# A decode attention kernel: most of each V tile's matmuls in a loop with register addresses, V tiles in two pieces of their own

## The chip, the cores and the metric

The kernel runs on one core of a Trainium2 chip. The metric is the time of one execution on the device in microseconds, as the median of several runs. The kernel before takes 2521.05 us, the median of 3 runs from 2520.66 to 2521.23. The profile is of one further execution, which took 2520.96 us; its span, from the first instruction to the last event, is 2519.1 us.

Names used below: TensorE (PE in the profile; PEld is its weight load), VectorE (DVE), ScalarE (ACT), GpSimd (POOL) and SyncE (SP), whose queue issues nearly all transfers here. SBUF is the on-chip memory that transfers write, PSUM the one that TensorE writes.

## The reference

One token goes through an attention block with a cached K and V and through a gated feed-forward block, and a scalar gate mixes the two.

```python
def _A_ref(x, k_cache, v_cache, wq, wo):          # x 1x1x512; caches 1 x 32 x 65536 x 128
    B, Sq, D = x.shape
    H, Dh = 32, 128
    q = (x @ wq).reshape(B, Sq, H, Dh).transpose(0, 2, 1, 3)
    scores = jnp.einsum("bhqd,bhkd->bhqk", q, k_cache) * (Dh ** -0.5)
    p = softmax(scores, axis=-1)
    o = jnp.einsum("bhqk,bhkd->bhqd", p, v_cache)
    return o.transpose(0, 2, 1, 3).reshape(B, Sq, H * Dh) @ wo

def _B_ref(x, w_gate, w_up, w_down):               # F = 1792
    return (silu(x @ w_gate) * (x @ w_up)) @ w_down

g = sigmoid((x * gate_w).sum(-1, keepdims=True))
return g * _A_ref(...) + (1 - g) * _B_ref(...)
```

All inputs are bf16. The two caches are 32 heads x 65536 keys x 128 numbers each, 537 MB apiece; each number is used once.

## The kernel before

**Tiles.** A head's 65536 keys lie as 512 keys on each of 128 partitions. A tile is half of that: 256 keys per partition (SIZE), 128 x 32768 bf16, 8.39 MB in one load. So a head has two K tiles and two V tiles (G = 2), and there are N = 64 of each. The loop over n (line 485) loads K tile n and V tile n-2 (LEAD = 2), in this order on SP's queue.

**A K tile** goes through VectorE in place (`products`, line 249): one multiply with the head's query row, which stands on all partitions (line 258), and three additions that fold the 128 numbers of a key to 16 (line 262: the 64-wide, 32-wide and 16-wide halves). TensorE sums the 16 with eight matmuls against the identity (`scores`, line 267), and VectorE takes the last pair together (`add_up`, line 282). At an even n the head before has all its scores: its maximum (`row_max`, line 299, with a step over ScalarE and TensorE), the exponentials on ScalarE and the weight 1/sum follow (`exponentials`, `weight`). They stand behind the multiply of the first 64 keys of K tile n; the other 192 keys follow as a second piece (cuts, line 497).

**A V tile** is used by `values` (line 335): 64 matmuls, each with four keys' probabilities as weights (128x4) and four keys' V rows (128 x 512) as the moving side. They go in turn to four strips of PSUM at partitions 0, 32, 64 and 96. When a head is complete, ScalarE copies O_ps to SBUF (`head_copy`), TensorE sums the useful rows (`head_sum`), and ScalarE writes the row, weighted, into a row of four heads (`head_row`, line 422). Every four heads, `turn` (line 461) turns the row to columns.

**Slots.** SBUF has three slots of a tile's size (`big0` to `big2`). K and V tiles and at the start and end the weights wq, the feed-forward weights and wo take the slot that came free first (`free`, lines 79 to 84). A K tile frees its slot after its scores (line 280), a V tile after its 64 matmuls (line 349). A load waits on SP's queue until its slot is free, and later loads wait behind it.

**wo.** The rows of wo for heads 0 to 3 are loaded during the run in 40 small loads (`load_tall`, line 395; TALL_LOADS, line 29) and multiplied then (`project_tall`). The others are loaded at the end, around the last two V tiles (lines 545 to 551): heads 4 to 19 ahead of the last V tile, the rest behind it.

**Order.** `manual_schedule()` (line 77) keeps each engine's instructions in the order of the program text. All addresses are constants and every loop is unrolled.

Of the kernel before, what the change touches and what calls it, by code (L numbers as in the profile page):

```python
# [8 lines left out]
ACT = mybir.ActivationFunctionType  # L9
# [6 lines left out]
SLOTS = 3  # L16
# [5 lines left out]
V_CUTS = {63: (0, 168, 232, 256)}  # L22

QUAD = 4
FIRST, LONG, PAIR, LAST = (0, 4), (4, 20), (20, 28), (28, 32)

SHARES = ((5, 3), (3, 15), (1, 4))
TALL_ROUNDS = ((2, 0, 4), (1, 0, 5), (1, 5, 10), (1, 10, 15), (0, 0, 3))
TALL_LOADS = {14: 0, 23: 1, 32: 2, 41: 3, 50: 4}
TALL_PROJECTS = {18: 0, 27: 1, 36: 2, 45: 3, 54: 4}  # L30
# [3 lines left out]
def kernel(  # L34
# [31 lines left out]
    qT = edge.tile([P, H], f32, name="qT")  # L66
    ring = ctx.enter_context(tc.tile_pool(name="ring", bufs=1))
    slots = [f"big{i}" for i in range(SLOTS)]
# [8 lines left out]
    ctx.enter_context(tc.manual_schedule())  # L77

    free = [2, 0, 1]
    taken = {}  # L80

    def big(name):
        slot = free.pop(0)
        return ring.tile([P, SIZE * Dh], bf16, name=name, tag=slots[slot]), slot

    wq_t, wq_slot = big("wq_t")
    wq_sb = wq_t[:, : KT * H * Dh].rearrange("p (t f) -> p t f", t=KT)
    nc.sync.dma_start(out=wq_sb, in_=A_wq.rearrange("(p t) f -> p t f", t=KT))  # L88
    x_row = consts.tile([1, D], bf16, name="x_row", tag="o_row")
    nc.scalar.dma_start(out=x_row, in_=A_x[0])  # L90

    K_tiles, V_tiles, S_tiles, P_tiles, S_parts = {}, {}, {}, {}, {}

    def load(dst, cache, n, name, cuts=None):
        t, taken[name, n] = big(name)
        view = t.rearrange("p (j d) -> p j d", d=Dh)
        src = cache[0, n // G, :, :].rearrange("(p j) d -> p j d", p=P)
        a = n % G * SIZE
        cuts = cuts or (0, SIZE)
        for c, d in zip(cuts[:-1], cuts[1:]):  # L100
            nc.sync.dma_start(out=view[:, c:d, :], in_=src[:, a + c : a + d, :])
        dst[n] = view
# [30 lines left out]
    def query_columns(first, last):  # L133
        q_ps = psum_m.tile([P, last - first], f32, name="q_ps", tag="misc")
        for h in range(first, last):
            for t in range(KT):
                nc.tensor.matmul(
                    q_ps[:, h - first : h - first + 1],
                    lhsT=wq_sb[:, t, h * Dh : (h + 1) * Dh],
                    rhs=xT[:, t : t + 1],  # L140
                    start=(t == 0),
                    stop=(t == KT - 1),
                )
        nc.scalar.activation(out=qT[:, first:last], in_=q_ps, func=ACT.Copy)
# [3 lines left out]
    def query_spread(h):  # L148
        diag_q = consts.tile([P, Dh], bf16, name="diag_q")
        nc.scalar.activation(out=diag_q, in_=ident_b, func=ACT.Copy, scale=qT[:, h : h + 1])  # L150
        qb_ps = psum_m.tile([P, Dh], f32, name="qb_ps", tag="misc")
        nc.tensor.matmul(qb_ps, lhsT=ones_b, rhs=diag_q, start=True, stop=True)  # L152
        q_tiles[h] = pair.tile([P, Dh], bf16, name="q_sb")
        nc.scalar.activation(out=q_tiles[h], in_=qb_ps, func=ACT.Copy)  # L154
# [3 lines left out]
    query_columns(0, 1)  # L158
    query_spread(0)
    query_columns(1, H)  # L160
    free.append(wq_slot)
# [10 lines left out]
    gu_t, gu_slot = ring.tile([P, SIZE * Dh], bf16, name="gu_t", tag=slots[wq_slot]), wq_slot  # L172
    free.remove(wq_slot)
# [5 lines left out]
    gw_row = consts.tile([1, D], bf16, name="gw_row", tag="tall")  # L179
# [69 lines left out]
    def products(n, a, b):  # L249

        K = K_tiles[n][:, a:b, :]
        qb = q_tiles[n // G]
        q_rep = bass.AP(
            tensor=qb.tensor,
            offset=qb.offset,
            ap=[list(qb.ap[0]), [0, b - a], [1, Dh]],
        )
        yield nc.vector.tensor_tensor(out=K, in0=K, in1=q_rep, op=ALU.mult)  # L258
# [75 lines left out]

    def values(n, lo=0, hi=SIZE):
        h = n // G
        a = n % G * SIZE
        for j in range(lo, hi, QUAD):
            strip = 32 * ((a + j) // QUAD % 4)
            nc.tensor.matmul(  # L340
                O_ps[strip : strip + QUAD, :],
                lhsT=P_tiles[h][:, a + j : a + j + QUAD],
                rhs=V_tiles[n][:, j : j + QUAD, :],
                start=(a + j < 4 * QUAD),
                stop=(a + j >= NBH - 4 * QUAD),
            )
        if hi == SIZE:
            del V_tiles[n]
            free.append(taken.pop(("V_t", n)))

    def head_copy():
        O_sb = consts.tile([P, QUAD * Dh], f32, name="O_sb")
        nc.scalar.activation(out=O_sb, in_=O_ps, func=ACT.Copy)  # L353
        return [O_sb[:, c * Dh : (c + 1) * Dh] for c in range(QUAD)]

    def head_sum(h, parts):
        if h >= LAST[0]:
            r_ps = psum_r.tile([P, 1], f32, name="r_ps")
            for c in range(QUAD):
                nc.tensor.matmul(  # L360
                    r_ps, lhsT=parts[c], rhs=pick[:, c : c + 1], start=(c == 0), stop=(c == 3)
                )
            return r_ps
        r_ps = psum_r.tile([1, Dh], f32, name="r_ps")
        for c in range(QUAD):
            nc.tensor.matmul(  # L366
                r_ps, lhsT=pick[:, c : c + 1], rhs=parts[c], start=(c == 0), stop=(c == 3)
            )
        return r_ps


    row0 = 0
    TP = 32 + 4 * SHARES[0][0]
    assert sum(2 * 4 * ports * deep for ports, deep in SHARES) == QUAD * P
    TR = max(b - a for _, a, b in TALL_ROUNDS)
    pieces, bases = [], []
    width = 0
    for ports, deep in SHARES:
        bases.append(width)
        for half in range(2):  # L380
            pieces.append((row0, row0 + 4 * ports * deep, width + 32 * half * deep))
            row0 += 4 * ports * deep
        width += TP * deep
    tallT = consts.tile([TP, sum(deep for _, deep in SHARES)], bf16, name="tallT")
    tall = {}

    def tall_row():
        tall["row"] = consts.tile([1, width], bf16, name="tall_row", tag="tall")
        nc.gpsimd.memset(tall["row"], 0.0)

    def tall_zero():
        tall["sb"] = consts.tile([TP, TR, D], bf16, name="tall_sb", tag="tall")
        nc.gpsimd.memset(tall["sb"], 0.0)

    def load_tall(r, half):
        s, a, b = TALL_ROUNDS[r]
        ports, deep = SHARES[s]
        first = pieces[2 * s + half][0]
        for i in range(4):
            src = bass.AP(  # L400
                tensor=A_wo.tensor,
                offset=A_wo.offset + (first + i * deep + a) * D,
                ap=[[4 * deep * D, ports], [1, (b - a) * D]],
            )
            lo = 32 * half + i
            nc.sync.dma_start(
                out=tall["sb"][lo : lo + 4 * (ports - 1) + 1 : 4, : b - a].rearrange(
                    "p t n -> p (t n)"
                ),
                in_=src,  # L410
            )

    def project_tall(r):
        s, a, b = TALL_ROUNDS[r]
        rows = 32 + 4 * SHARES[s][0]
        at = sum(deep for _, deep in SHARES[:s])
        for t in range(b - a):
            into_row(tallT[:rows, at + a + t : at + a + t + 1], tall["sb"][:rows, t, :])
# [3 lines left out]
    def head_row(h, r_ps):  # L422
# [4 lines left out]
        if h < FIRST[1]:  # L427
            for a, b, at in pieces:
                lo, hi = max(a, h * Dh), min(b, h * Dh + Dh)
                if lo < hi:  # L430
                    nc.scalar.activation(
                        out=tall["row"][:, at + lo - a : at + hi - a],
                        in_=r_ps[:, lo - h * Dh : hi - h * Dh],
                        func=ACT.Copy,
                        scale=gate[0:1, :],
                    )
            return
        if h % QUAD == 0:
            rows[h // QUAD] = consts.tile([1, QUAD * Dh], bf16, name="o_row")
        at = (h % QUAD) * Dh  # L440
        nc.scalar.activation(
            out=rows[h // QUAD][:, at : at + Dh], in_=r_ps, func=ACT.Copy, scale=gate[0:1, :]
        )

    def turn_first():
        t_ps = psum_m.tile([TP, tallT.shape[1]], f32, name="t_ps", tag="misc")
        c = 0
        for s, (ports, deep) in enumerate(SHARES):
            src = tall["row"][:, bases[s] : bases[s] + TP * deep]
            for t in range(deep):  # L450
                nc.tensor.matmul(
                    t_ps[:, c + t : c + t + 1],
                    lhsT=src.rearrange("o (p t) -> o t p", t=deep)[:, t, :],
                    rhs=one_b,
                    start=True,
                    stop=True,
                )
            c += deep
        nc.scalar.activation(out=tallT, in_=t_ps, func=ACT.Copy)

    def turn(g):
        if g == 0:
            turn_first()
            return
        first, last = LONG if g * QUAD < LONG[1] else PAIR
# [154 lines left out]
```

## Time and profile before

| what | value |
|---|---|
| median of 3 runs | 2521.05 us |
| the profiled execution | 2520.96 us, span 2519.1 us |
| VectorE busy | 2185.8 us, 87% |
| TensorE matmuls busy | 698.7 us, 28% |
| ScalarE busy | 95.1 us, 4% |
| read from HBM | 1087.64 MB, 432 GB/s over the span |
| instructions in the profile | 12218 |
| instruction fetch (queue q8) | 42 packets, 0.69 MB |
| mean granted TensorE clock | 0.613 of full speed |

How to read the profile: the page has the busy time of each engine, the span cut in 40 slices with a digit for the busy share of each (9 is 90% or more), and the chain of waits that ended last. A row of the timeline has the start and the duration in us, the engine, the line of the kernel, the operation, the tile that is written and those that are read, the shapes and the count; in brackets stand the idle time before it and what ended it. Rows of the view by form have, after the count, the sum in us, the mean of one in ns and the idle time before. In the shape of a matmul, 128*4 is the weights' and 128x512 the moving side's. SPq is a load being issued on SP's queue, not its transfer.

### The profile page before, as it was taken

To read this page: it belongs to the slowest core of one execution; us is meant where nothing else is said; L and a number is where in the kernel's file an instruction comes from. 1 tells how busy PE (TensorE), PEld (TensorE's weight loads), DVE (VectorE), ACT (ScalarE), POOL (GpSimd) and SP (SyncE) were. 2 spreads that over 40 slices of the span, in tenths; PEclk is the share of its full clock that TensorE was granted. 3 is DMA by queue.
4 is the path that set the end of the run, shared out by engine and by line. 5 is a ranking of instruction groups with operands and counts; after the bars stand their busy time and mean duration, and the time that the engine had idled before them with its cause. 6 is when DMAs were issued, how large, how long until landed. Compare 5 with 4: busy or idle time off the path is not lost.

```text
span 2519.1 us, 12218 instructions
## 1 busy us (share of the span) xinstructions
PE 698.7 (28%) x5422; PEld 252.0 (10%) x5422; DVE 2185.8 (87%) x599; ACT 95.1 (4%) x277; POOL 4.0 (0%) x8
## 2 busy tenths in 40 slices
PE   2132222223222222232222322322323223223224
PEld 2010000101001000010000100110100001001011
DVE  6998998888988889888899888898888988889984
ACT  0000000000000000000000000000000000000000
POOL 0000000000000000000000000000000000000000
PEclk9566556656566566665665665656555666656566
DMA  9999999999999999999999999999999999999998
GB/s 419 435 433 433 437 437 433 432 433 435 432 433 434 434 433 433 435 434 433 434 437 432 432 433 433 434 433 434 434 434 433 434 434 433 434 436 432 432 432 378
DMA packets 20875, 1088.41 MB, mean 432 GB/s; under 512 B 2396, under 2 KB 2912, under 8 KB 3416
## 3 DMA queue, kind: packets, MB, share of 16 engines
q1 hardware_dynamic: 20822, 1087.65, 99.7%
q8 instruction: 42, 0.69, 0.1%
q14 instruction: 9, 0.07, 0.0%
q10 hardware_dynamic: 2, 0.00, 0.0%
HBM read 1087.64 MB, written 0.00 MB: 432 GB/s over the span
## 4 chain that ended last, share of the span: by engine, by line
DMA 84%; PE 14%; DVE 1%; issue 0%; SPq 0%; ACT 0%; DVEq 0%
DMA V_t<-in_A_v_cache_dram 81%; PE O_ps L340 14%; DMA wo_t<-in_A_wo_dram 2%; DMA K_t<-in_A_k_cache_dram 1%; DVE K_t L258 1%; DVE K_t L262 1%; PE part_ps L271 0%; PE b_ps L227 0%; SPq L88 0%; ACT out_sb L588 0%; PE a_ps L186 0%; PE g_ps L231 0%; DVEq L258 0%
## 5 line engine op out<-in xcount | busy, mean ns | idle before, releaser
L258 DVE TENSOR_TENSOR K_t<-K_t,q_sb 128x8192 bf16<-128x8192 bf16 (+4 forms) x97 | 1107.3, 11416 | 245.2 <-DMA K_t<-in_A_k_cache_dram 245.2
L262 DVE TENSOR_TENSOR K_t<-K_t 128x4096 bf16<-128x4096 bf16 (+8 forms) x291 | 1001.5, 3441 | 9.0
L340 PE MATMUL O_ps<-V_t,P_sb 128*4 128x512 bf16 x4096 | 365.5, 534 | 923.9 <-DMA V_t<-in_A_v_cache_dram 923.8
L271 PE MATMUL part_ps<-K_t,ident_b 128*128 128x512 bf16 x512 | 230.6, 605 | 611.1 <-DVE K_t L262 611.1
L340 PEld LDWEIGHTS <-P_sb 128*4 128x4 bf16 x4096 | 122.7, 110 | 1160.7 <-issue 1075.5
L271 PEld LDWEIGHTS <-ident_b 128*128 128x128 bf16 x512 | 59.9, 117 | 753.0 <-issue 752.9
L306 PE MATMUL mT_ps<-diag,ones_f 128*128 128x129 f32 (+1 forms) x64 | 25.3, 497 | 215.9 <-ACT diag L303 215.9
L287 DVE TENSOR_REDUCE S_sb<-part_ps 128x256 f32<-128x512 f32 x64 | 43.7, 683 | 3.5 <-PE part_ps L271 3.5
L313 DVE TENSOR_REDUCE top<-mT_ps 128x1 f32<-128x128 f32 x32 | 9.3, 291 | 42.1 <-PE mT_ps L306 42.1
L154 ACT ACTIVATE q_sb<-qb_ps 128x128 bf16<-128x128 f32 x32 | 8.9, 277 | 940.2 <-PE qb_ps L152 940.2
L353 ACT ACTIVATE O_sb<-O_ps 128x512 f32<-128x512 f32 x31 | 18.4, 595 | 581.4 <-PE O_ps L340 581.4
L366 PE MATMUL r_ps<-O_sb,pick 128*1 128x128 f32 x224 | 40.3, 341 | 0.0
L306 PEld LDWEIGHTS mT_ps<-diag,ones_f 128*128 128x128 f32 x64 | 15.8, 307 | 227.1 <-ACT diag L303 227.1
L303 ACT ACTIVATE diag<-ident_b,m 128x128 f32<-128x128 bf16 x32 | 12.8, 401 | 577.3 <-DVE m L301 577.3
L366 PEld LDWEIGHTS r_ps<-O_sb,pick 128*1 128x1 f32 x224 | 20.3, 100 | 32.5 <-issue 22.5
L317 ACT ACTIVATE P_sb<-S_sb,bias 128x512 bf16<-128x512 f32 x32 | 23.1, 722 | 1.2
L301 DVE TENSOR_REDUCE m<-S_sb 128x1 f32<-128x512 f32 x32 | 22.0, 686 | 1.1
L574 DVE TENSOR_SCALAR fold<-O_ps,pick 128x128 f32<-128x128 f32 x1 | 0.4, 351 | 23.4 <-PE O_ps L340 23.4
L201 PE MATMUL gu_ps<-xT,gu_t 128*128 128x1 bf16 x112 | 7.0, 198 | 21.2 <-DMA gu_t<-in_B_w_gate_dram 20.5
L150 ACT ACTIVATE diag_q<-ident_b,qT 128x128 bf16<-128x128 bf16 x32 | 12.3, 385 | 0.0
L201 PEld LDWEIGHTS <-gu_t 128*128 128x128 bf16 x112 | 6.9, 158 | 21.4 <-DMA gu_t<-in_B_w_gate_dram 20.6
L186 PE MATMUL a_ps<-b_sb,ones_f 1*1 1x256 f32 x4 | 1.0, 606 | 28.6 <-ACT b_sb L245 28.6
(68 smaller groups left out, 112.6 us busy)
## 6 DMA issues: line engine op xcount, KB each, us to landing
K_t<-in_A_k_cache_dram SPq DMA_DIRECT2D x2, 4096.0 KB
V_t<-in_A_v_cache_dram SPq DMA_DIRECT2D x1, 5376.0 KB
K_t<-in_A_k_cache_dram SPq DMA_DIRECT2D x1, 5120.0 KB
wq_t<-in_A_wq_dram SPq DMA_DIRECT2D x1, 4096.0 KB
K_t<-in_A_k_cache_dram SPq DMA_DIRECT2D x1, 3072.0 KB
wo_t<-in_A_wo_dram SPq DMA_DIRECT2D x1, 2048.0 KB
V_t<-in_A_v_cache_dram SPq DMA_DIRECT2D x1, 2048.0 KB
gu_t<-in_B_w_gate_dram SPq DMA_DIRECT2D x1, 1792.0 KB
```

Of the source, the lines that this page charges most:

```text
L201: nc.tensor.matmul(gu_ps[:, w * FT + ft : w * FT + ft + 1], lhsT=cols[:, t, ft, :], rhs=xT[:, t : t + 1], start=(t == 0), stop=(t == KT - 1),)
L258: yield nc.vector.tensor_tensor(out=K, in0=K, in1=q_rep, op=ALU.mult)
L262: yield nc.vector.tensor_tensor(out=K[:, :, 0:half], in0=K[:, :, 0:half], in1=K[:, :, half : 2 * half], op=ALU.add,)
L271: nc.tensor.matmul(part, lhsT=ident_b, rhs=K_tiles[n][:, :, c : c + wide], start=(c == 0), stop=(c == WIDTH - wide),)
L287: nc.vector.tensor_reduce(out=S_tiles[h][:, a : a + SIZE], in_=S_parts.pop(n), axis=AXIS.X, op=ALU.add)
L301: nc.vector.tensor_reduce(out=m, in_=S_tiles[h], axis=AXIS.X, op=ALU.max)
L303: nc.scalar.activation(out=diag[:, :P], in_=ident_b, func=ACT.Copy, scale=m)
L306: nc.tensor.matmul(mT_ps[:, :wide], lhsT=ones_f, rhs=diag[:, :wide], start=True, stop=True)
L317: nc.scalar.activation(out=P_tiles[h], in_=S_tiles[h], func=ACT.Exp, bias=bias, scale=scale, accum_out=new_sum(h),)
L340: nc.tensor.matmul(O_ps[strip : strip + QUAD, :], lhsT=P_tiles[h][:, a + j : a + j + QUAD], rhs=V_tiles[n][:, j : j + QUAD, :], start=(a + ...
L353: nc.scalar.activation(out=O_sb, in_=O_ps, func=ACT.Copy)
L366: nc.tensor.matmul(r_ps, lhsT=pick[:, c : c + 1], rhs=parts[c], start=(c == 0), stop=(c == 3))
```

## The change

**The slots.** K tiles alternate between two slots of a whole tile. V tiles have two buffers of their own: `long` for 208 keys (LOOPED), `short` for 48. A V tile n-2 is two loads. The weights wq, the feed-forward weights and wo use `long`.

**The loop.** For V tiles 0 to 59 (UNROLLED), `values_begun` puts the matmuls of the long piece into a loop on TensorE, four to a turn, whose counter gives the address of weights and V rows through registers. All of the loop's matmuls go to strip 0. For the first tile of a head the first 16 keys are unrolled ahead of it, in four strips. The short piece's 12 matmuls stay unrolled behind it, in four strips. The loop stands in `tc.tile_critical()`, a block of its own in the program with an entry and an exit.

**Where it stands.** In the text of tile n the loop comes behind the softmax of the head before (even n) and ahead of what is left of K tile n on VectorE; the load of the short piece follows. In the built program VectorE's stream has the whole multiply and the first addition of K tile n ahead of the branch that separates the blocks, and SP's stream the short piece's load. TensorE's stream has, at the block's entry, waits for the counters of all engines and load queues up to these instructions, and behind the loop a drain, on which the next long piece's load waits. A turn of the loop is four matmuls with register addresses, four instructions that each work out several address sums, an addition and a compare-and-branch; for the second tile of a head four further register additions.

**The rest.** The query is computed as rows (four partitions, 1024 numbers each) instead of columns, and spread with one matmul without the diagonal copy. Two heads are summed at once. Rows of five or four heads are turned. wo has no early rows: the piece ahead of the last V tile is heads 0 to 19. At an even n the multiply is cut in two halves of 128 keys, with the softmax of the head before in between, and the additions run over all 256 keys.

```diff
-SLOTS = 3
-FIRST, LONG, PAIR, LAST = (0, 4), (4, 20), (20, 28), (28, 32)
-SHARES = ((5, 3), (3, 15), (1, 4))
...
+LONG, PAIR, LAST = (0, 20), (20, 28), (28, 32)
+GROUPS = ((0, 5), (5, 10), (10, 15), (15, 20), (20, 24), (24, 28))
+UNROLLED = 60
+LOOPED, TURN = 208, 4
...
-    ctx.enter_context(tc.manual_schedule())
-    free = [2, 0, 1]
+    ctx.enter_context(tc.manual_schedule(engines={ET.PE, ET.DVE, ET.Activation, ET.SP}))
+    free = [0, 1]
...
+    def load_part(n, last):
+        c, d = (LOOPED, SIZE) if last else (0, LOOPED)
+        t = ring.tile([P, SIZE * Dh - LOOPED * Dh], bf16, name="V_b", tag="short") if last else long_part("V_a")
+        V_parts[n, last] = t.rearrange("p (j d) -> p j d", d=Dh)
+        src = A_v_cache[0, n // G, :, :].rearrange("(p j) d -> p j d", p=P)
+        a = n % G * SIZE
+        nc.sync.dma_start(out=V_parts[n, last], in_=src[:, a + c : a + d, :])
...
-        yield nc.vector.tensor_tensor(out=K, in0=K, in1=q_rep, op=ALU.mult)
+        for c in range(parts):
+            k = K[:, c * some : (c + 1) * some, :]
+            yield nc.vector.tensor_tensor(out=k, in0=k, in1=q_rep, op=ALU.mult)
...
+    def four_keys(n, j, strip, start=False, stop=False):
+        a = n % G * SIZE
+        nc.tensor.matmul(
+            O_ps[32 * strip : 32 * strip + QUAD, :],
+            lhsT=P_tiles[n // G][:, bass.ds(j + a, QUAD)],
+            rhs=keys_of(n, j),
+            start=start,
+            stop=stop,
+        )
+
+    def values_begun(n):
+        group, step = 4 * QUAD, TURN * QUAD
+        begin = 0 if n % G else group
+        values(n, 0, begin)
+        with tc.tile_critical():
+            with nc.tensor.Fori(begin, LOOPED - step + 1, step) as j:
+                for c in range(TURN):
+                    four_keys(n, j + c * QUAD if c else j, 0)
+
     def values(n, lo=0, hi=SIZE):
...
+        first, group = n % G == 0, 4 * QUAD
         for j in range(lo, hi, QUAD):
...
+            four_keys(n, j, j // QUAD % 4, first and j < group, not first and j >= SIZE - group)
...
         if v is not None:
-            load(V_tiles, A_v_cache, v, "V_t")
-            for half in range(2):
-                if n - half in TALL_LOADS:
-                    load_tall(TALL_LOADS[n - half], half)
+            begun = v < UNROLLED
+            load_part(v, False)
+            if not begun:
+                load_part(v, True)
...
             exponentials(top_of, row_max(top_of))
+        if v is not None and begun:
+            values_begun(v)
+            load_part(v, True)
         for _ in vector:
             pass
...
         if v is not None:
-            values(v)
+            values(v, LOOPED if begun else 0)
```

`keys_of` returns the V rows of four keys, out of the long or the short piece.

More of the change, by code (lines that the diff above doesn't have):

```diff
@@ L65 @@
     ident_b = edge.tile([P, P], bf16, name="ident_b")
-    qT = edge.tile([P, H], f32, name="qT")
+    q_rows = edge.tile([97, H * Dh // 4 + Dh // 2], bf16, name="q_rows")
     ring = ctx.enter_context(tc.tile_pool(name="ring", bufs=1))
-    slots = [f"big{i}" for i in range(SLOTS)]
     consts = ctx.enter_context(tc.tile_pool(name="consts", bufs=1))
@@ L143, in query_columns @@
                 )
[L144 removed]
+        for i in strips:
+            nc.scalar.activation(
+                out=q_rows[32 * i : 32 * i + 1, c * BANK : (c + 1) * BANK],
+                in_=q_ps[c][32 * i : 32 * i + 1, :],
+                func=ACT.Copy,
+            )
     q_tiles = {}
     def query_spread(h):
[L149 to L150 removed]
+        i, at = h * Dh // q_wide, h * Dh % q_wide
         qb_ps = psum_m.tile([P, Dh], f32, name="qb_ps", tag="misc")
[L152 removed]
+        nc.tensor.matmul(
+            qb_ps,
+            lhsT=ones_b[32 * i : 32 * i + 1, :],
+            rhs=q_rows[32 * i : 32 * i + 1, at : at + Dh],
+            start=True,
+            stop=True,
+        )
         q_tiles[h] = pair.tile([P, Dh], bf16, name="q_sb")
@@ L333, in weight, with head_copy, head_sum @@
         nc.vector.tensor_tensor(out=rg[:, h : h + 1], in0=recip, in1=gval, op=ALU.mult)
+    def four_keys(n, j, strip, start=False, stop=False):
+        a = n % G * SIZE
+        nc.tensor.matmul(
+            O_ps[32 * strip : 32 * strip + QUAD, :],
[3 more added lines that the diff above has]
+            stop=stop,
+        )
+    def values_begun(n):
[6 more added lines that the diff above has]
+                    four_keys(n, j + c * QUAD if c else j, 0)
     def values(n, lo=0, hi=SIZE):
-        h = n // G
-        a = n % G * SIZE
+        first, group = n % G == 0, 4 * QUAD
         for j in range(lo, hi, QUAD):
[L339 to L356, printed above, removed]
+            four_keys(n, j, j // QUAD % 4, first and j < group, not first and j >= SIZE - group)
+    def head_copy(h):
+        if h % 2 == 0 or h >= LAST[0]:
+            O_sbs[0] = consts.tile([P, 2, QUAD * Dh], f32, name="O_sb")
+        both = O_sbs[0]
+        nc.scalar.activation(out=both[:, h % 2, :], in_=O_ps, func=ACT.Copy)
+        return both
+    O_sbs = {}
+    def head_sum(h, both):
         if h >= LAST[0]:
@@ L384 @@
[L384 to L418, printed above, removed]
+                r_ps,
+                lhsT=pick[:, c : c + 1],
+                rhs=both[:, :, c * Dh : (c + 1) * Dh],
+                start=(c == 0),
+                stop=(c == QUAD - 1),
+            )
+        return r_ps
     rows = {}
@@ L440, in head_row @@
[L440 to L465, printed above, removed]
+        if r_ps is None:
+            return
+        for k in (h - 1, h):
+            first = [a for a, b in GROUPS if a <= k < b][0]
+            if k == first:
+                rows[first] = pair.tile([1, 5 * Dh], bf16, name="o_row")
+            at = (k - first) * Dh
+            nc.scalar.activation(
+                out=rows[first][:, at : at + Dh],
+                in_=r_ps[:, (k - h + 1) * Dh : (k - h + 2) * Dh],
+                func=ACT.Copy,
+                scale=rg[0:1, k : k + 1],
+            )
```

138 lines of the change are left out of this document (64 added, 74 removed).

## The prediction

> **What bounds the kernel now.** I read the page first, its slices and its chain of waits, then the timeline of two neighbouring tiles from the middle of the run.
>
> ```profile
> DMA  9999999999999999999999999999999999999998
> ...
> DMA 84%; PE 14%; DVE 1%; issue 0%; SPq 0%; ACT 0%; DVEq 0%
> ```
>
> Every slice has the DMA engines busy, and the chain is DMA. PE's 14% is the V matmul that frees a slot; the load issued then queues behind a running one, so this share costs nothing. The timeline shows by how much:
>
> ```profile
> 1208.42 17.23 DVE L258 TENSOR_TENSOR K_t<-K_t,q_sb 128x32768 bf16<-128x32768 bf16 x1 [2.04 <-DMA K_t<-in_A_k_cache_dram]
> 1225.68 15.48 DVE L262 TENSOR_TENSOR K_t<-K_t 128x16384 bf16<-128x16384 bf16 x3
> 1227.76 6.38 PE L340 MATMUL O_ps<-V_t,P_sb 128*4 128x512 bf16 x64 [17.66 <-DMA V_t<-in_A_v_cache_dram]
> 1234.19 0.33 SPq L101 DMA_DIRECT2D V_t<-in_A_v_cache_dram  x1
> 1241.21 3.60 PE L271 MATMUL part_ps<-K_t,ident_b 128*128 128x512 bf16 x8 [7.07 <-DVE K_t L262]
> ...
> 1247.31 4.43 DVE L258 TENSOR_TENSOR K_t<-K_t,q_sb 128x8192 bf16<-128x8192 bf16 x1 [5.56 <-DMA K_t<-in_A_k_cache_dram]
> 1251.66 0.69 DVE L287 TENSOR_REDUCE S_sb<-part_ps 128x256 f32<-128x512 f32 x1
> ...
> 1254.87 4.28 DVE L262 TENSOR_TENSOR K_t<-K_t 128x4096 bf16<-128x4096 bf16 x3
> ...
> 1266.57 5.76 PE L340 MATMUL O_ps<-V_t,P_sb 128*4 128x512 bf16 x64 [12.21 <-DMA V_t<-in_A_v_cache_dram]
> ```
>
> V lands at 1227.76, its 64 matmuls end at 1234.14, and the next V load is issued at 1234.19, while the K load ahead of it lands only at 1247.3: 13 us of cover. V tiles' matmuls start 38.6 us apart (38.57 to 38.90, and 39.9 to 40.1 four times); that is one K and one V tile of 8.39 MB each at 434 GB/s, 19.3 us a piece. DVE idles 5.56 and 2.0 us for K in each pair. So any edit short of a hole in the load queue is free.
>
> **The change, part by part.** The heart is where a V tile's long piece is freed. In the built program the matmul loop of tile n (it works on V tile n-2) stands behind a block entry where TensorE waits for the counters of every engine and every load queue. The counts named there include the short piece of the same V tile and, on DVE, the second instruction after the softmax work: the whole multiply and the first (64-wide) addition of K tile n. The next long piece's load waits until the loop is over. Count from the landing of K tile n:
>
> DVE, odd n: one multiply 17.23 and one addition 8.69 (by-form row below): 25.9 us. Even n: the first 128 keys' multiply 8.68 (the two 128x16384 instructions of that line), then the reduces, maximum and weight, 1251.66 to 1254.87 in the timeline, 3.3 with its gap; the second multiply 8.68; the addition 8.69: 29.4 us. In the kernel before, the matmuls started when V had landed, 19.3 us after K.
>
> ```profile
> L262 DVE TENSOR_TENSOR K_t<-K_t 128x16384 bf16<-128x16384 bf16 x31 | 269.4, 8692 | 1.1
> ...
> L258 DVE TENSOR_TENSOR K_t<-K_t,q_sb 128x16384 bf16<-128x16384 bf16 x2 | 17.4, 8677 | 0.0
> ...
> L340 PEld LDWEIGHTS <-P_sb 128*4 128x4 bf16 x4096 | 122.7, 110 | 1160.7 <-issue 1075.5 <-ACT P_sb L317 54.7
> ```
>
> The loop: 48 matmuls for even n (16 keys go ahead of it), 52 for odd, all into strip 0, where before four strips ran side by side. One 512-column matmul alone takes 0.427 us in the slow state (eight scores matmuls in 3.60). The bursts of 64 average 5.71 us (4.7 to 6.6); sixteen groups of four at 0.427 would be 6.8, so the clock doubles on the way. From 0.427g + 0.2135(16-g) = 5.71, g is 10.7 groups: 4.6 us slow, then 0.2135 a group. In one strip: 4.6 + (48-10.7) x 0.2135 = 12.5 us. The shortest burst gives 11.5, no speed-up at all 20.5. [...]
>
> No row shows register instructions, of which a turn of four matmuls has 6 (even) or 10 (odd), branch included. Below, they cost nothing: line 137 issues 124 pairs of weight load and matmul in 3.49 us, 14 ns an instruction, and a turn's matmuls give 0.85 us of cover. Above, at the 0.33 us that SP's sequencer takes to issue a load, an even turn takes 2.0 us and the loop 24, an odd one 3.3 and 43. Between them lies the weight load in line: a register-addressed matmul stands in the built program without a separate weight load, and at the row's 0.110 each the loop is 12.5 + 48 x 0.110 = 17.8. I take the middle of 12.5 and 17.8, 15.0 (odd 16.2), since the loop's work is PE's own rows.
>
> The stall: in the steady stream the next long piece would start 38.6 us after K n landed (V n-2 and K n+1 lie between). It can start at 29.4 + 15.0 + 0.7 (block entry and exit; an estimate, two of SP's 0.33) + 2.0 (a load into an idle queue: x_row needs 1.3 us from issue to its reader, the output 2.5 to the end of the span) = 47.1. So the queue is empty for 8.5 us once a pair. The odd loop follows with 25.9 + 16.2 + 2.7 = 44.8 against 38.6 + 8.5: no stall of its own. 30 even loops (V tiles 0 to 58): 255 us. The first comes later still, since DVE begins K tile 2 at 91.6 and not at its landing (85.1): 6 us once.
>
> The rest. Queries as rows: 32 matmuls of 512 columns in place of 128 of one column (3.8 us); at 0.427 in strips of four that is about 3.4 plus 1.7 for head 0, hidden, for DVE waits until 21.90 for K and the weight loads behind line 175 have K tile 0 ahead of them. The diagonal copies (32 x 0.385 on ScalarE) and half the head sums' matmuls go; both lie in idle time. The even tiles' multiplies and additions in other cuts: 17.4 us either way, additions 15.5 for 16.0, with the maximum 4 us later in the tile; that lateness is in the 29.4. Two slots for K in place of a rotation of three: K n-2 is freed about 50 us after its landing (29.4 + 15.0 + 0.7, the short piece's 12 matmuls, 3.6 of scores), the next load into it begins at 3 x 19.3 = 58. wo without early rows: 40 small loads fewer on SP's queue (2.79 us of issue for four; the tile after such loads came 38.81 for 38.6 us), 2 us in all, which a queue with holes gives nothing back for; 0.5 MB more at the end, 1.2 us at 434 GB/s, and eight matmuls more under the 9.17 us in which TensorE waits for the last V tile. DVE, ScalarE, SP and GpSimd each branch once a loop: DVE's is past the addition that the loop waits for, and a pair that grows leaves DVE over 7 us idle, so up to some us each stay hidden.
>
> Sum: 2519.1 + 255 + 6 + 1 = 2781 of span; the profiled execution had 2520.96 for 2519.1, so 2783. Its 2520.96 stands within 0.1 us of the median, 2521.05.
>
> **The rivals.** (1) TensorE's sequencer, not the array, paces the loop. In rows: the 42 instruction packets are 16 KB, and a bulk packet (1087.65 MB in 20822) is 52 KB, 1.93 us at a sixteenth of 432 GB/s; one such wait a turn makes the loop 23.2 us and the stall 16.7: 2519 + 501 + 7 + 2 = 3029. For it: nothing here shows a branch's price. Against it: the body is at most 14 instructions. [...] No row decides. At 0.33 us an instruction the odd loop (43 us) would rule, and the time passes 3500.
>
> (2) Not slower: the entry lets TensorE in when V has landed, because the counts on DVE are reached by then. Then the loop ends 19.3 + 15.0 + 2.7 = 37.0 us after K, under 38.6: no hole, DMA bounds, and 2 us of small loads and 0.3 MB of instructions (0.8 us) come back: 2518. It decides where entry comes before 20.9 us after K landed. Against it: 25.9 and 29.4 are sums of plain rows.
>
> (3) Matmuls of one strip overlap, so that the loop takes some 9 us: stall 2.5, 2519 + 75 + 7 + 2 = 2603. Against it: line 227 puts 14 matmuls of 512 columns into one strip in 3.33 us, 0.238 each.
>
> That the change doesn't do what it says is out: the loops stand in the built program.
>
> **How the numbers follow.** Forecast 0.76, rival 1 0.13, rival 2 0.05, rival 3 0.06. The forecast's own ends: a loop of 11.5 us gives stalls of 5.0 and 2678, one of 20.5 gives 14.0 and 2948. The range, 2650 to 2990, adds a little to each side for the nearer part of rivals 1 and 3; some 0.19 stays outside. About 0.2% (5 us) is what a measurement can tell from no change: faster 0.02, same 0.04 (rival 2), slower 0.94.
>
> **What would show it.** Right: the V_a loads' issue waits for TensorE, not for a load; DMA holes near 8 us once in two tiles, GB/s near 390; the loop's first matmul right behind the first addition of K; the loop 12 to 18 us; DVE idle before K about doubled. Wrong: loops that begin when V lands, holes at both tiles of a pair, or a loop whose matmuls stand over 0.43 us apart.

## The result, and the profile after

| | before | after |
|---|---|---|
| median | 2520.86 us (4 runs, 2520.64 to 2521.23) | 2792.34 us (4 runs, 2790.83 to 2793.07) |
| span of the profiled execution | 2519.1 us | 2791.3 us |
| instructions in the profile | 12218 | 18556 |
| instruction fetch (q8) | 0.69 MB | 0.39 MB |

The ratio is 1.1076, with a 95% interval of 1.1057 to 1.1095: the changed kernel is 271 us slower. The forecast was 2783 us, with a range from 2650 to 2990.

First the page of the changed kernel: the 40 slices of the DMA engines' busy share and of the bytes moved, and the bulk queue (packets, MB, share of the 16 engines).

```profile
DMA  9898998988998889989899898898989998989899
GB/s 424 353 421 372 384 422 384 385 376 382 429 387 373 382 377 419 392 361 388 376 408 404 366 387 383 383 420 377 390 369 382 423 384 383 390 378 427 365 400 385
...
q1 hardware_dynamic: 29510, 1087.65, 91.4%
...
DMA 4%; PE 0%; ACT 0%; issue 0%
```

The same queue in the kernel before:

```profile
q1 hardware_dynamic: 20822, 1087.65, 99.7%
```

The bytes are the same as before, but the queue worked 91.4% of the span where it had worked 99.7%, and the rate swings between about 430 and 360 GB/s. The last line of the first block is the chain of waits. It covers 4% of the span and goes no further back than the last loops, so the cause has to be read from the waits. The next lines are waits (us in total, times, longest): two of the changed kernel's engines, VectorE's wait for K in the kernel before, and SP's queue in the changed kernel.

```profile
PE O_ps L371 <- DVE K_t L296: 853.5, 55, 26.8
DVE K_t L292 <- DMA K_t<-in_A_k_cache_dram: 513.3, 62, 17.9
```

```profile
DVE K_t L258 <- DMA K_t<-in_A_k_cache_dram: 245.2, 61, 19.4
```

```profile
SPq L110 <- PEq L383: 1852.8, 60, 40.1
```

TensorE waits at the loops for VectorE (L296 is the additions), VectorE waits 513 us for K (245 before), and 60 issues on SP's queue, one a loop, wait for TensorE's sequencer at L383, which is the exit of the block. The timeline shows where this leaves the queue empty (rows from an even tile, at 1214, to the end of the next odd one):

```profile
1214.25 0.69 DVE L321 TENSOR_REDUCE S_sb<-part_ps 128x256 f32<-128x512 f32 x1 [2.12 <-PE part_ps L305]
...
1225.87 15.47 DVE L296 TENSOR_TENSOR K_t<-K_t 128x16384 bf16<-128x16384 bf16 x3
...
1235.33 13.36 PE L371 MATMUL O_ps<-V_a,P_sb 128*4 x48 [6.74 <-DVE K_t L296]
...
1248.94 0.33 SPq L110 DMA_DIRECT2D V_a<-in_A_v_cache_dram  x1
...
1252.68 17.23 DVE L292 TENSOR_TENSOR K_t<-K_t,q_sb 128x32768 bf16<-128x32768 bf16 x1 [11.33 <-DMA K_t<-in_A_k_cache_dram]
...
1269.94 15.47 DVE L296 TENSOR_TENSOR K_t<-K_t 128x16384 bf16<-128x16384 bf16 x3
1279.49 9.35 PE L371 MATMUL O_ps<-V_a,P_sb 128*4 x28 [26.05 <-DVE K_t L296]
...
1292.16 8.69 DVE L292 TENSOR_TENSOR K_t<-K_t,q_sb 128x16384 bf16<-128x16384 bf16 x1 [6.15 <-DMA K_t<-in_A_k_cache_dram]
...
1297.22 0.33 SPq L110 DMA_DIRECT2D V_a<-in_A_v_cache_dram  x1
```

Behind the even loop the long piece is issued at 1248.94, 3.7 us before the K load that runs at the time lands (1252.68). Behind the odd loop it is issued at 1297.22, 5.1 us after K landed (1292.16): the queue has nothing to do from 1292.16 on. The view by stretches shows the same; its last two numbers are the DMA engines' busy share and the GB/s moved:

```profile
1292.00:1298.10 6.10, 5.13 (x29) 1.54 (x29) 5.94 (x1) 0.00 (x0) 0.00 (x0) 1.00 0.00 0
```

The odd loop makes the hole. (The first row of the timeline is VectorE waiting for scores, for the section on the forecast.)

I call the distance from a multiply that starts on the landing of K to the next such multiply a tile's time. From K tile 10 on (the first is tile 0) it is 46.3 us on average from an even K to the odd one behind it and 40.0 from an odd K to the even one, 86.32 a pair; before, a pair took 77.27 (median). This and the later means are taken over some 26 tiles of each kind from there on. The 272.2 us between the spans (2791.3 - 2519.1) are made up so: K tile 4 starts 13.3 us later than before (175.75 for 162.43), the 29 pairs from there to K tile 62 take 251 us more, 8.66 each, and the rest to the end takes 7.8 us more. That is less than 86.32 - 77.27 a pair, as the first pairs lose less and the kernel before loses some time at four places of its own (next section).

### The profile page after: what moved, and what is told of

Same layout as the page of the kernel before. It is cut to its first block, busy times and chain, and to the rows that moved or that the text cites. A ratio compares the mean times of both kernels' runs of the same rounds, so it can differ in the third digit from the quotient of the medians.

```text
span 2791.3 us, 18556 instructions
## 1 busy us (share of the span) xinstructions
PE 1245.1 (45%) x5172; PEld 393.8 (14%) x5172; DVE 2175.6 (78%) x506; ACT 89.2 (3%) x245; POOL 0.7 (0%) x6
## 3 DMA queue, kind: packets, MB, share of 16 engines
q1 hardware_dynamic: 29510, 1087.65, 91.4%
## 5 line engine op out<-in xcount | busy, mean ns | idle before, releaser
L292 DVE TENSOR_TENSOR K_t<-K_t,q_sb 128x16384 bf16<-128x16384 bf16 (+2 forms) x97 | 1107.4, 11417 | 513.3 <-DMA K_t<-in_A_k_cache_dram 513.3
L371 PE MATMUL O_ps<-V_a,P_sb 128*4 (+1 forms) x3224 | 876.1, 438 | 1370.3 <-DVE K_t L296 853.5
L296 DVE TENSOR_TENSOR K_t<-K_t 128x16384 bf16<-128x16384 bf16 (+5 forms) x198 | 987.0, 4985 | 6.8
L371 PEld LDWEIGHTS O_ps<-V_a,P_sb 128*4 x3000 | 270.1, 90 | 1600.1 <-issue 1447.1
L305 PE MATMUL part_ps<-K_t,ident_b 128*128 128x512 bf16 x512 | 230.4, 605 | 29.4 <-DVE K_t L296 29.4
L371 PEld LDWEIGHTS <-P_sb 128*4 128x4 bf16 x1096 | 25.9, 87 | 414.5 <-issue 353.4
L305 PEld LDWEIGHTS <-ident_b 128*128 128x128 bf16 x512 | 51.3, 110 | 175.6 <-issue 175.5
L371 PE MATMUL O_ps<-V_b,P_sb 128*4 128x512 bf16 x744 | 50.8, 378 | 12.6 <-PEq L383 12.6
L340 PE MATMUL mT_ps<-diag,ones_f 128*128 128x129 f32 (+1 forms) x64 | 17.8, 365 | 55.9 <-ACT diag L337 55.1
L418 PE MATMUL r_ps<-O_sb,pick 128*1 128x256 f32 x112 | 26.4, 378 | 0.0
L555 DVE TENSOR_SCALAR fold<-O_ps,pick 128x128 f32<-128x128 f32 x1 | 0.3, 350 | 23.5 <-PE O_ps L371 23.5
L371 PE MATMUL O_ps<-V_t,P_sb 128*4 128x512 bf16 x128 | 11.2, 504 | 10.5 <-DMA V_t<-in_A_v_cache_dram 10.5
L217 PE MATMUL a_ps<-b_sb,ones_f 1*1 1x256 f32 x4 | 1.0, 606 | 29.8 <-ACT b_sb L276 29.8
## 6 DMA issues: line engine op xcount, KB each, us to landing
K_t<-in_A_k_cache_dram SPq DMA_DIRECT2D x1, 5120.0 KB, 30.7
wq_t<-in_A_wq_dram SPq DMA_DIRECT2D x1, 4096.0 KB, 12.3
```

What stands on the lines that cost most here:

```text
L292: yield nc.vector.tensor_tensor(out=k, in0=k, in1=q_rep, op=ALU.mult)
L296: yield nc.vector.tensor_tensor(out=K[:, :, 0:half], in0=K[:, :, 0:half], in1=K[:, :, half : 2 * half], op=ALU.add,)
L305: nc.tensor.matmul(part, lhsT=ident_b, rhs=K_tiles[n][:, :, c : c + wide], start=(c == 0), stop=(c == WIDTH - wide),)
L340: nc.tensor.matmul(mT_ps[:, :wide], lhsT=ones_f, rhs=diag[:, :wide], start=True, stop=True)
L371: nc.tensor.matmul(O_ps[32 * strip : 32 * strip + QUAD, :], lhsT=P_tiles[n // G][:, bass.ds(j + a, QUAD)], rhs=keys_of(n, j), start=start, ...
L418: nc.tensor.matmul(r_ps, lhsT=pick[:, c : c + 1], rhs=both[:, :, c * Dh : (c + 1) * Dh], start=(c == 0), stop=(c == QUAD - 1),)
```

## The experiments

The first run removes all loops and blocks, the next seven change a part of the loops, the blocks or the entry, and the last joins two of these edits. Medians of the kernel before beside them: 2520.98 to 2521.10.

### No loops, no blocks

```diff
-UNROLLED = 60
+UNROLLED = 0
```

> No loop and no block: all V tiles' matmuls unrolled in four strips behind the scores work, the rest of the change kept (the V pieces in slots of their own, two slots for K, queries as rows, multiplies and additions in the new cuts, wo without early rows). Theory (the block's wait and the loop's length make the hole, and the other parts are hidden): the loads are the bound again, 2516 to 2522 us, some 2 us of it won or lost by the wo rows. Rival (the smaller reserve of slots or the two pieces cost by themselves): over 2540 us, with idle time of the load queue left between tiles.

Measured: 2523.65 us, ratio to before 1.001 (1.0001 to 1.0019). That is 1.7 us above the range expected, and far below the rival's 2540. The slices are full again:

```profile
DMA  9999999999999999999999999999999999999998
...
q1 hardware_dynamic: 29510, 1087.65, 99.8%
```

So 269 of the 271 us hang on the loops and their blocks. The rest of the change costs 2.5 us, where the forecast's sum had 1 us. By the starts of the multiplies, 1.3 to 1.5 us are won at four places where the kernel before loads rows of wo; about 1 of it is lost again two or three tiles later each time, and 0.6 to 0.8 at four further places, so that the last K tile is 3.1 us late. What costs this was not taken apart.

### The block with a short inside

```diff
         with tc.tile_critical():
-            with nc.tensor.Fori(begin, LOOPED - step + 1, step) as j:
-                for c in range(TURN):
-                    four_keys(n, j + c * QUAD if c else j, 0)
+            for j in range(begin, LOOPED, QUAD):
+                four_keys(n, j, j // QUAD % 4)
```

> The block with its entry, its exit and its waits stays at its place; inside it 48 or 52 matmuls stand unrolled with constant addresses and in four strips, so the loop's 12 to 18 us become about 5. Theory: entry 29.4 us after K landed at even n (25.9 at odd n), plus 0.8, 5 and 0.2 is 35.4, under 38.6, so no hole: 2516 to 2530 us. Rival (the block's entry and exit stop the engines and cost by themselves, whatever stands inside): 2600 us or more.

Measured: 2548.68 us, ratio 1.0104 (1.0091 to 1.0118). Neither theory has this number: the block costs no 80 us, but 25 us more than nothing. At even n the issue comes 35.0 us after K's landing, as the theory had it (35.4); that an issue under 38.6 costs nothing is what was wrong. Two pairs of this kernel, with the issue of a long piece and the two multiplies around it:

```profile
829.82 0.33 SPq L110 DMA_DIRECT2D V_a<-in_A_v_cache_dram  x1
...
833.16 17.23 DVE L292 TENSOR_TENSOR K_t<-K_t,q_sb 128x32768 bf16<-128x32768 bf16 x1 [2.61 <-DMA K_t<-in_A_k_cache_dram]
...
873.40 8.69 DVE L292 TENSOR_TENSOR K_t<-K_t,q_sb 128x16384 bf16<-128x16384 bf16 x1 [6.90 <-DMA K_t<-in_A_k_cache_dram]
...
1220.04 0.33 SPq L110 DMA_DIRECT2D V_a<-in_A_v_cache_dram  x1
...
1224.73 17.23 DVE L292 TENSOR_TENSOR K_t<-K_t,q_sb 128x32768 bf16<-128x32768 bf16 x1 [3.45 <-DMA K_t<-in_A_k_cache_dram]
...
1263.43 8.69 DVE L292 TENSOR_TENSOR K_t<-K_t,q_sb 128x16384 bf16<-128x16384 bf16 x1 [5.36 <-DMA K_t<-in_A_k_cache_dram]
```

In the first the issue is 3.3 us ahead of K's landing, and the next tile takes 40.2 us; in the second it is 4.7 us ahead, and the tile takes 38.7, as in the steady stream. So a load that was issued before the queue was empty still cost time here, 40.2 - 38.6 = 1.6 us in the first pair. The last section has this for all runs.

### The block with unrolled matmuls of one strip, and the same without the block

```diff
         with tc.tile_critical():
-            with nc.tensor.Fori(begin, LOOPED - step + 1, step) as j:
-                for c in range(TURN):
-                    four_keys(n, j + c * QUAD if c else j, 0)
+            for j in range(begin, LOOPED, QUAD):
+                four_keys(n, j, 0)
```

> The block stays; inside it the 48 or 52 matmuls stand unrolled with constant addresses, all into strip 0 as in the loop. Theory (the loop's length counts; the array paces the even loop, the register work the odd one): even about 13.2 us as before, odd 14 in place of 17.7; then the even tile's chain rules (41.8 us from the issue of the long piece to K landed, 29.4 on VectorE, 0.8 entry, 13.2 loop, 0.2: 85.4 a pair for 86.3), 2735 to 2770 us. Rival (addresses in registers and the loop's branch are the cost): back to about 2521 us. Rival (the even tile gates anyway, as predicted, at 15 us): within 10 us of 2792.

Measured: 2756.88 us, ratio 1.0933 (1.0918 to 1.0948). Constant addresses give only 35 us back. The even stretch takes 12.5 us from its first to its last weight load, the odd one 12.5 where the odd loop took 17.3. Now the long piece is issued 4.1 us after K's landing behind the even block and 6.5 us ahead of it behind the odd one: the gate, the loop that makes the hole, has moved to the even tile.

In the second of the two the line `with tc.tile_critical():` goes too.

> No block: the same unrolled strip-0 matmuls at the same place in TensorE's stream, with constant addresses. Theory (the wait at the entry is one half of the cause): they start when the long piece has landed, 15.7 us after K, and end by 15.7 + 14 = 30, under 38.6: no hole, 2516 to 2525 us. Rival (the serial strip alone is the cost): 2700 us or more.

Measured: 2523.56 us, ratio 1.001 (1.0001 to 1.0019), as with four strips. The same serial matmuls start when the long piece has landed, and cost nothing:

```profile
1209.91 17.23 DVE L292 TENSOR_TENSOR K_t<-K_t,q_sb 128x32768 bf16<-128x32768 bf16 x1 [2.88 <-DMA K_t<-in_A_k_cache_dram]
...
1225.63 12.83 PE L371 MATMUL O_ps<-V_a,P_sb 128*4 128x512 bf16 x50 [14.73 <-DMA V_a<-in_A_v_cache_dram]
...
1238.92 0.33 SPq L110 DMA_DIRECT2D V_a<-in_A_v_cache_dram  x1
...
1248.60 8.69 DVE L292 TENSOR_TENSOR K_t<-K_t,q_sb 128x16384 bf16<-128x16384 bf16 x1 [5.35 <-DMA K_t<-in_A_k_cache_dram]
```

They start 15.7 us after K landed (1225.63 - 1209.91), and the next long piece is issued 9.7 us ahead of the next K's landing. With the three runs above: the long stretch alone is free, the block alone costs 25 us, both together cost 233.

### The entry earlier

```diff
-            yield nc.vector.tensor_tensor(
-                out=K[:, :, 0:half], in0=K[:, :, 0:half], in1=K[:, :, half : 2 * half],
-                op=ALU.add,
-            )
+            fine = 4 if half == 64 and b - a == SIZE else 1
+            step = (b - a) // fine
+            for c in range(0, b - a, step):
+                k = K[:, c : c + step, :]
+                yield nc.vector.tensor_tensor(
+                    out=k[:, :, 0:half], in0=k[:, :, 0:half], in1=k[:, :, half : 2 * half],
+                    op=ALU.add,
+                )
```

> The first (64-wide) addition of each K tile is cut into four pieces of 64 keys. In the built program two of them (odd n) or one (even n) stand ahead of the block, where the whole addition stood: the entry waits 4.3 us less at odd n and 6.5 us less at even n; the work on VectorE is the same. Theory (TensorE waits at the entry for VectorE's count, and that wait sets the period): the odd chain, 86.4 a pair, becomes 82.1, 31 pairs: 2640 to 2680 us. Rival (TensorE is held by the loop, the branches or the loads, not by VectorE): within 15 us of 2792.

Measured: 2665.97 us, ratio 1.0572 (1.0555 to 1.0590). The loops are the same (12.3 and 17.3 us); their first weight load comes 22.6 us after K landed at odd n (26.8 in the changed kernel), a pair takes 82.17 us for 82.1 expected:

```profile
1197.08 17.22 DVE L292 TENSOR_TENSOR K_t<-K_t,q_sb 128x32768 bf16<-128x32768 bf16 x1 [8.48 <-DMA K_t<-in_A_k_cache_dram]
1214.34 15.68 DVE L300 TENSOR_TENSOR K_t<-K_t 128x4096 bf16<-128x4096 bf16 x6
1219.69 7.99 PE L375 MATMUL O_ps<-V_a,P_sb 128*4 x24 [25.00 <-DVE K_t L300]
```

The loop starts while the additions (L300 here) still run, 0.9 us behind the second quarter: two quarters take 4.5 us (a half of the 64-wide addition's 8.69, with the cut), which ends at 1218.8. In the timeline of the changed kernel the odd loop starts the same 0.9 us behind the whole addition (1269.94 + 8.69 = 1278.63, and 1279.49). At odd n the wait at the entry is for VectorE's count, and each microsecond of it is one of the period: 4.2 us less of wait, 4.15 less a pair.

### The odd loop without its register additions

```diff
     def four_keys(n, j, strip, start=False, stop=False):
-        a = n % G * SIZE
+        a = n % G * SIZE if isinstance(j, int) else 0
```

> In the odd loops the probabilities of the first 256 keys are used in place of the second 256 (the output changes there), so that the offset of the second half and its four register additions a turn go; all else as changed. Theory (the odd loop is paced by TensorE's register work and gates since it takes 17.7 us): the odd loop falls to 12.5 to 14 us, as the even one; then the even tile's chain rules and the time is that of the block with unrolled strip-0 matmuls, 2745 to 2775 us. Rival (the even loop gates anyway, as predicted): within 10 us of 2792.

Measured: 2751.71 us, ratio 1.0911 (1.0893 to 1.0929). The odd loop falls to 12.9 us and the pair to 85.07 (85.27 with constant addresses): without the four additions a loop with register addresses runs nearly as fast as unrolled matmuls of one strip (12.9 for 12.5). The issue behind the even loop is now 4.3 us late, that behind the odd one 5.4 us ahead.

### A shorter loop

```diff
-LOOPED, TURN = 208, 4
+LOOPED, TURN = 176, 4
```

> 176 in place of 208 keys in the loop: 40 matmuls at even n, 44 at odd n, and 20 unrolled ones behind. Theory (each looped matmul costs its own time): odd loop 15.0 for 17.7 us, even 11.5 for 13.2, so a pair about 2.6 us shorter: 2690 to 2735 us. Rival (a fixed price of each block or each V piece): within 20 us of 2792.

Measured: 2708.45 us, ratio 1.0746 (1.0728 to 1.0764). The odd loop has 44 matmuls for 52 and takes 14.6 us for 17.3; the pair takes 83.58 for 86.32. Both differences are 2.7 us. (In this build the even entry also stands ahead of the 64-wide addition. The even loop then starts 25.8 us after K on average, about 1 us behind the landing of the short piece, 1193.43 for 1192.29: the entry waits for that load too. The odd chain, which sets the period, is unchanged but for the loop.)

### Two matmuls to a turn

```diff
-LOOPED, TURN = 208, 4
+LOOPED, TURN = 208, 2
```

> Two matmuls to a turn in place of four, so twice as many turns, each with its addition and its compare-and-branch; the matmuls and their address sums stay as many. In the trace of the changed kernel the odd loop's weight loads have gaps of 0.17 us in a turn and 0.53 us at its end. Theory (the end of a turn costs 0.36 us more than a step in it, and that is seen wherever the array does not cover it): odd loop 26 turns of 0.86 us, 22.4 us, 4.7 us more a pair: 2900 to 2980 us; the even loop grows if two matmuls (0.43 us) do not cover a turn's end. Rival (only the four register additions cost): within 15 us of 2792.

Measured: 2946.12 us, ratio 1.1687 (1.1668 to 1.1707). The odd loop takes 22.3 us and the even one 16.1. The weight loads show the turns, first an odd loop of the changed kernel, then an odd and an even one of this kernel (start, duration, and in brackets the gap before):

```profile
1290.41 0.08 PEld L371 LDWEIGHTS O_ps<-V_a,P_sb 128*4 x1 [0.53 <-issue]
1290.66 0.08 PEld L371 LDWEIGHTS O_ps<-V_a,P_sb 128*4 x1 [0.17 <-issue]
...
1291.78 0.08 PEld L371 LDWEIGHTS O_ps<-V_a,P_sb 128*4 x1 [0.53 <-issue]
```

```profile
1269.55 0.08 PEld L371 LDWEIGHTS O_ps<-V_a,P_sb 128*4 x1 [0.53 <-issue]
1269.80 0.08 PEld L371 LDWEIGHTS O_ps<-V_a,P_sb 128*4 x1 [0.17 <-issue]
1270.45 0.08 PEld L371 LDWEIGHTS O_ps<-V_a,P_sb 128*4 x1 [0.57 <-issue]
...
1311.31 0.23 PEld L371 LDWEIGHTS O_ps<-V_a,P_sb 128*4 x2 [0.44 <-issue]
1312.02 0.23 PEld L371 LDWEIGHTS O_ps<-V_a,P_sb 128*4 x2 [0.48 <-issue]
```

An odd turn of four is 1.37 us (1290.41 to 1291.78), an odd turn of two 0.88 (1269.55 to 1272.20 is three). So a matmul with its addition takes 0.245 us and the turn's end 0.39. The even turn of two is 0.69 on average: two loads 0.15 apart, as in the row's 0.23 for two of 0.08, and again 0.39 for the end. So the end of a turn costs, as the theory had it, and the rival falls; a register addition costs too, 0.245 - 0.15, about 0.1 us.

### Earlier entry and lean odd loop together

> Both edits together: the 64-wide addition in four pieces (entry earlier) and the odd loops without their four register additions (they use the probabilities of the first 256 keys, so the output changes there). Theory (period = the longer of two chains, each from a long piece's issue over two tiles' transfers to VectorE's count, the loop and the next issue): odd 21.6 + 0.8 + 13 + 0.2 = 35.6 us and even about 24.5 + 12.6 + 0.2 = 37.3 us after K landed, under 38.6, so no whole hole is left; but the block with short matmuls showed that an issue only 3 to 5 us ahead of the end of the queue still loses 0 to 2 us, so 1 to 5 us a pair remain: 2550 to 2650 us. Rival (the two savings overlap, only the larger counts): 2666 us, as the cut addition alone. Rival (a queue that is never empty loses nothing): 2523 us.

Measured: 2593.12 us, ratio 1.0289 (1.0272 to 1.0306). The odd loop starts 22.6 us after K landed and takes 13.1, the even one 23.5 and 12.2. Both issues are ahead of K's landing, by 3.7 and 3.3 us, and still a pair takes 79.71 us, 2.4 more than before: neither rival holds. The gains of the two edits alone are 126 and 41 us; together they give 199: the lean loop alone left the even tile as the gate, the earlier entry alone the odd one.

No version beats the kernel before; the two without blocks come within 0.1% of it.

## Why the forecast held, and what in it did not

**The chain was right.** Entry behind the first addition of K, a serial loop, an issue that waits for the exit, a queue that runs dry once a pair: the waits on SP's queue, the earlier entry and the shorter loop each show a link of it, and taking away either the block or the long stretch brings 2524 or 2549 us.

**The gate was the wrong one.** "The odd loop follows with 25.9 + 16.2 + 2.7 = 44.8 against 38.6 + 8.5: no stall of its own" is the step that failed. The forecast let the even loop make the hole, by 29.4 + 15.0 + 0.7 = 45.1 us from K's landing to the issue, against 42.8 at odd n. Measured means:

| from K's landing | even n, forecast | even n, measured | odd n, forecast | odd n, measured |
|---|---|---|---|---|
| to the first weight load of the loop | 29.4 and half of 0.7 | 30.7 | 25.9 and half of 0.7 | 26.8 |
| first to last weight load | 15.0 | 12.05 | 16.2 | 17.3 |
| to the issue of the next long piece | half of 0.7 | 0.7 | half of 0.7 | 0.5 |
| sum | 45.1 | 43.5 | 42.8 | 44.6 |
| issue, seen from the next K's landing | 6.5 us late (45.1 - 38.6) | 2.9 us ahead | 4.3 us ahead (47.1 - 42.8) | 4.6 us late |

At 43.5 us the even loop ends ahead of the next landing because that landing is late itself: it comes 46.3 us after the even K, behind the hole that the odd loop before has made. Each of the two chains comes back to itself after a pair, and the longer one sets the period: with a restart of 3.1 us (below) and two tiles' transfers, 44.6 + 3.1 + 38.6 = 86.3 us by the odd loop and 43.5 + 3.1 + 38.6 = 85.2 by the even one. In the first pairs the even loop did make a hole, as forecast: behind K tile 4 its issue is 3.2 us late, at tile 6 0.9, and from tile 8 on it is ahead, but for one tile. The forecast's own terms give 45.1 + 2.0 + 38.6 = 85.7 by the even loop and 83.4 by the odd one. That 2783 lies so near to 2792 is therefore luck in part: the wrong loop's chain had nearly the right length.

**Terms that were mis-sized and cancelled.** The forecast took 15.0 us as the middle between 12.5 (register work hidden) and 17.8 (weight load in line). Each loop came out near one end: the even loop 12.05, the odd one 17.3, and not for the reason named: its excess is the four register additions with the turn's end. The restart was put at 2.0 us. Behind the odd loop the issue comes 4.6 us late and the tile is 46.3 - 38.6 = 7.7 us longer, so the restart is 3.1; and behind the even loop an issue 2.9 us ahead still costs 40.0 - 38.6 = 1.4. VectorE's wait for scores in an even tile, 2.12 us in the first row of the timeline above, comes from the odd loop's lateness and was no term of the forecast; on average it is worth 0.9, since the even loop starts 29.8 us after K in the unrolled block of one strip, whose odd stretch is shorter, and 30.7 here. Together a pair loses 8.66 us on average for 8.5, and the first hole is 13.3 us for 8.5 + 6.

**The clock.** In the even loop at 1235.33 the weight loads stand 0.43 us apart for most of the first 5.9 us and 0.216 apart for the other 33. Over the 26 even loops the slow part takes 4.05 us on average, from 2.8 to 6.2. The forecast's estimate from the bursts of the kernel before was 4.6 us, and 12.5 for the loop; the loop's mean, 12.05 us and 0.2 for the last matmul, comes near that, but the slow part is shorter here on average and varies, and with it the loop (11.55 to 12.95 us).

**The rivals.** The one that TensorE's sequencer paces the loop holds for the odd loop, at 1.37 us a turn and not at the 1.93 us that it priced; instruction fetch is not its cause, for q8 moved 0.39 MB in place of 0.69. The rival that the entry lets TensorE in when V has landed is what happens without the block (15.7 us after K landed). The rival of overlapping matmuls falls: one strip takes 12.5 us unrolled as well, where it priced 9.

**The rest of the change** was put at 1 us in the sum; without the loops it costs 2.5 us.

## What to carry to other kernels

The loop in a block of its own took its place in other engines' orders here (TensorE waited 853.5 us at the loops for VectorE, SP's queue 1852.8 us for the exits): before putting one in, look in the built program which instructions of other engines stand ahead of the block, and add their durations to the release of every buffer that the loop reads. With a single buffer behind such a release, count from the landing that starts the chain to the next issue, and leave some 6 to 8 us until the queue runs dry (0.2 us lost with that lead here, 1.1 with 3 to 4 us: the table below). Where two kinds of turn alternate, cost them apart: here the longer one gated, and a saving on it ended where the other took over (4.4 us off the odd loop gave 1.25 us a pair).

## What the runs showed of the hardware

**In these runs a tile took longer the later its V load was issued, from 0.2 us more at 6 to 12 us ahead of the queue's end to 8.0 at 4 to 5 us behind it.** The rows give the mean excess of a tile over 38.57 us (a steady tile of the kernel before) by the moment of the V issue, counted from the start of the multiply on the K load ahead of it, each from the run that it names:

| issue | excess of the tile | tiles |
|---|---|---|
| 9 to 12 us ahead (one strip, no block) | 0.2 us (0 to 1.5) | 48 |
| 6 to 8 us ahead (block with a short inside) | 0.2 us (-0.2 to 0.9) | 13 |
| 4 to 5 us ahead (joined edits) | 0.5 us (0 to 1.1) | 12 |
| 3 to 4 us ahead (block with a short inside) | 1.1 us (0.2 to 3.6) | 21 |
| 2 to 3 us ahead (changed kernel) | 2.1 us (0.1 to 4.4) | 8 |
| 0 to 1 us late (earlier entry) | 3.3 us | 5 |
| 1 to 2 us late (earlier entry) | 4.7 us | 19 |
| 4 to 5 us late (block with one strip, unrolled) | 8.0 us | 18 |

The same lead costs somewhat differently by run: 3 to 4 us ahead means 0.9 us in the changed kernel and 1.5 with the joined edits. Beyond the end of the queue the excess is the lateness and 3.0 to 3.7 us on average, by run.

The records of the single transfers in the traces show where most of this lies. Behind the odd loops of the changed kernel the new load's first transfer starts 0.95 to 0.97 us after the start of its issue, the middle one of its first 16 transfers 1.1 us after it. At the other end, the 16 transfers of 4 bytes that close the K load come 1.6 us before VectorE starts on it, on average, and the last of them 0.4 us before. So 2.7 of some 3.1 us are accounted for; the rest is open. The spread of these ends also explains a part of what an early issue loses: in the block with a short inside the first of them comes 2.8 us before VectorE starts, and fewer than 16 transfers run from then until the next load has begun. With the issue 3.7 us ahead, the mean behind its even blocks, the share that stands idle comes to 0.3 us of the 1.0 us lost.

**What a loop costs TensorE's sequencer** could be read from its own rows with two matmuls to a turn: 0.15 us between two weight loads with register addresses, some 0.1 us for a register addition, 0.39 us for the end of a turn. An even turn of four would be 0.99 us by these prices, more than the array's 0.86 (four times 0.216), yet no gap shows in the 33 loads of the loop at 1235.33. The other even loops of the changed kernel fit a sequencer that gets ahead while the array is slow and uses this up later: in the 12 loops with the shortest slow part (2.8 to 3.35 us) weight loads stand over 0.35 us apart at the end of one or more later turns, in the other 14 nowhere behind the slow part. Here are the last two turns' ends of the loop at 975.38, whose slow part takes 2.9 us (the gap before each turn stands in brackets):

```profile
985.40 0.58 PEld L371 LDWEIGHTS O_ps<-V_a,P_sb 128*4 x4 [0.31 <-issue]
986.42 0.54 PEld L371 LDWEIGHTS O_ps<-V_a,P_sb 128*4 x4 [0.44 <-issue]
```
